# ScalarE in written order in the loop, its normalisation and its decoding cut into parts, weight loads on its queue

## The chip, the cores and the metric

The kernel runs on one core of a Trainium2 chip. The core has a matrix engine (TensorE, PE in the profile, with its weight loads as PEld), a vector engine (VectorE, DVE), a scalar engine (ScalarE, ACT), a general engine (GpSimd, POOL) and a queue engine that mostly issues transfers (SyncE, SP). Each engine takes its instructions in the order of its own queue. The metric is the device time of one execution in microseconds.

## The reference, cut to what matters

Attention with a decay per head (no softmax), then two MLPs; all in float32, the weights come as float64.

```python
scores = scale * np.matmul(q, k.transpose(0, 1, 3, 2))      # 4 x 8 heads, 576 x 64
ret = scores * Dmat[None, :, :, :]                          # gamma ** (i - j), lower triangle
x = np.matmul(ret, v)                                       # -> 2304 tokens x 512

h = x @ w_in                                                # 512 -> 1024
e = np.exp(h - h.max(-1)); sm = e / (e.sum(-1) + 1e-9)
solu = h * sm
ln = (solu - mu) / np.sqrt(var + 1e-6) * g_ln
x = ln @ w_out                                              # 1024 -> 512

h = x @ w_in2                                               # 512 -> 2048
g = np.where(h >= 1, h, np.where(h <= -1, 0.0, (h + 1) ** 2 / 4))
out = g @ w_out2                                            # 2048 -> 512
```

## The kernel before

The 2304 tokens are 18 tiles of 128. Every float32 operand of a product is split into a high part and a low part (`split`, L73: ScalarE copies the high part, VectorE subtracts), and a product is three matmuls.

The program has three stages. **START** is a table of steps that carries the attention ahead by six tiles, prepares the first MLP's weights and begins on the first two tokens' hidden layer. **The loop** (L507) runs over pairs of token tiles a = 2j and a + 1, j = 1 to 8: transposes of the normalised tile a-2 (`mlp1_transpose`, `tp`), scores of the attention of tile ra, the two halves of the hidden layer of tile a (`mlp1_hidden`, `hp`, 12 matmuls each), its normalisation (`mlp1_norm`), the transposes of a-1, the attention output of ra (`ret_out`), the same for a+1, and the first MLP's output of the pair before (`mlp1_out`, `px`). Attention runs until the fifth pair. The text calls j = 1 the first pair, and so on. **The last stage** is the second MLP.

In between, in the loop, the weights of the second MLP are prepared in 32 steps (`prep_w2`): a load of 512 KB (`prep_load`, `st`), `decode` of the float64 words into float32 (ScalarE L197 and L198, VectorE's shift L199, GpSimd's addition L200, VectorE's sign L202), and the split into `wi` (first matrix) or, after two loads, GpSimd's four combinations in `ws` (L366) and the split into `wo` (second matrix, in two parts). The results go to DRAM (`wid`, `wod`) and are loaded again in the last stage. `PACE` says how many steps stand at each of four places of a pair. The stage's loads have three buffers (`st`).

Normalisation of a tile: VectorE takes the two halves' maxima (L255) and their minimum (L261, the maxima are negated); ScalarE exponentiates (`e<-hp`, L265); VectorE multiplies with `hp` (`e<-hp,e`, L266), the last reader of `hp`; ScalarE squares into `junk` (L273); GpSimd takes the power and the bias (L279, L280); ScalarE writes the normalised `e` (L283), which the transposes read. `hp` has two buffers of PSUM (tag "h") in pairs one to five; the odd tiles from 13 on use another tag.

Order: in the loop TensorE and SP are pinned to the written order (L506). VectorE, ScalarE and GpSimd are ordered by a list scheduler.

## Time and profile before

| | |
|---|---|
| runs | 724.83, 729.98, 730.9 us; median 729.98 |
| profiled execution | 727.76 us, of which the span is 726.0 |
| busy: PE, DVE, ACT, POOL | 688.2, 497.1, 359.8, 169.7 us |
| mean granted clock of TensorE | 0.979 |
| START / first pair / pairs two to five / six to eight / last stage | 74.10 / 39.35 / 144.30 / 71.52 / 396.73 us |

TensorE is the busiest engine; busy time is counted over the whole span, and the stages are unlike. A wait counts where the engine that waits is the one that the end depends on. The granted clock is given as a share of 2.4 GHz; 0.5 is 1.2 GHz.

### The profile page before, as it was taken

How to read it: one execution, taken by the hardware profiler on the slowest of the kernel's cores; microseconds unless marked ns; L12 is line 12 of the kernel's file. 1: busy time of each engine (PE TensorE's matmuls, PEld its weight loads, DVE VectorE, ACT ScalarE, POOL GpSimd, SP SyncE). 2: the span in 40 equal slices, each digit the busy share in tenths (PEclk: the TensorE clock that was granted, in tenths of full speed). 3: DMA queues.
4: the chain of work that ended last, by engine and by line, in shares of the span. 5: the costliest groups of instructions: out<-in, count | busy, mean ns of one | idle time of the engine just before them, and what ended most of it. 6: DMA issues, size and time to landing. Idle time of an engine off the chain costs nothing.

```text
span 726.0 us, 12169 instructions
## 1 busy us (share of the span) xinstructions
PE 688.2 (95%) x4744; PEld 618.5 (85%) x4744; DVE 497.1 (68%) x961; ACT 359.8 (50%) x658; POOL 169.7 (23%) x186
## 2 busy tenths in 40 slices
PE   5888789998989999999999999999999999999997
PEld 4677578887878889999888989898988899899996
DVE  2977777677588678754566578556865668575875
ACT  2746775575667569763434344333433343343342
POOL 2896645636555235400000000000000000000000
PEclk9989899999999999999999999999999999999999
DMA  8956534487869399699564523346135511555282
GB/s 299 373 185 250 186 116 157 152 324 245 299 224 340 128 356 394 242 391 402 178 242 143 190 89 144 137 184 218 47 125 192 203 59 59 203 193 196 77 320 116
DMA packets 34825, 152.05 MB, mean 209 GB/s; under 512 B 3792, under 2 KB 11984, under 8 KB 29008
## 3 DMA queue, kind: packets, MB, share of 16 engines
q1 hardware_dynamic: 34624, 151.02, 56.8%
q8 instruction: 37, 0.61, 0.3%
q10 hardware_dynamic: 144, 0.26, 0.1%
q14 instruction: 20, 0.16, 0.1%
HBM read 114.04 MB, written 37.22 MB: 208 GB/s over the span
## 4 chain that ended last, share of the span: by engine, by line
PE 72%; DVE 11%; DMA 6%; ACT 4%; POOL 3%; issue 3%; SPq 0%; DVEq 0%; POOLq 0%; ACTq 0%
PE h L414 27%; PE hp L250 9%; PE px L316 7%; PE pa L462 7%; PE pb L462 7%; PE pc L462 7%; PE pd L462 3%; DMA st<-in_w_out 2%; POOL y L200 2%; PE po L149 1%; DMA wod<-wo 1%; PE tp L296 1%; DVE y L199 1%; DVE wo L75 1%; DVE p L124 1%
## 5 line engine op out<-in xcount | busy, mean ns | idle before, releaser
L414 PE MATMUL h<-xs,wi 128*128 128x512 f32 (+1 forms) x960 | 214.2, 372 | 0.0
L414 PEld LDWEIGHTS h<-xs,wi 128*128 128x128 f32 x960 | 163.8, 188 | 28.5
L424 DVE SCALAR_TENSOR_TENSOR r<-r 128x512 f32<-128x512 f32 (+1 forms) x80 | 50.8, 635 | 104.0 <-ACT r L422 103.9
L422 ACT ACTIVATE r<-h 128x512 f32<-128x512 f32 (+1 forms) x80 | 44.4, 555 | 154.7 <-PE h L414 154.6
L74 ACT ACTIVATE gh<-gs 128x1024 fp32r<-128x1024 f32 (+1 forms) x80 | 66.9, 874 | 77.1 <-DVE gs L437 72.9
L316 PE MATMUL px<-ln,wo 128*128 128x256 f32 x864 | 101.4, 278 | 0.0
L316 PEld LDWEIGHTS px<-ln,wo 128*128 128x128 f32 x864 | 100.5, 188 | 0.8 <-ACT e L265 0.2
L250 PE MATMUL hp<-wi1h,x 128*128 128x512 f32 x288 | 96.3, 417 | 0.0
L75 DVE TENSOR_TENSOR gl<-gs,gh 128x1024 fp32r<-128x1024 f32 (+1 forms) x80 | 77.1, 995 | 13.3 <-ACT gh L74 13.2
L200 POOL TENSOR_TENSOR y<-y,st 128x512 int32<-128x512 int32 x48 | 64.2, 1340 | 70.6 <-ACT st L198 22.9
L250 PE MATMUL hp<-wi1l,x 128*128 128x512 f32 x144 | 62.7, 435 | 14.6 <-DVE e L266 12.6
L462 PE MATMUL pb<-wo,gh 128*128 128x256 f32 x288 | 73.9, 280 | 0.4 <-DVE x L75 0.4
L250 PEld LDWEIGHTS hp<-wi1h,x 128*128 128x128 f32 x288 | 58.6, 203 | 13.4
L437 DVE TENSOR_TENSOR gs<-gs 128x256 f32<-128x256 f32 (+1 forms) x160 | 60.0, 396 | 3.6
L462 PE MATMUL pa<-wo,gh 128*128 128x256 f32 x288 | 62.5, 280 | 0.0
L462 PE MATMUL pc<-wo,gh 128*128 128x256 f32 x288 | 62.0, 280 | 0.0
L429 DVE TENSOR_TENSOR gs<-h,r 128x512 f32<-128x512 f32 (+1 forms) x80 | 51.1, 638 | 7.3 <-DVE r L424 0.5
L462 PEld LDWEIGHTS pb<-wo,gh 128*128 128x128 f32 x288 | 54.3, 188 | 0.6 <-issue 0.6
L462 PEld LDWEIGHTS pa<-wo,gh 128*128 128x128 f32 x288 | 49.2, 189 | 2.7
L462 PEld LDWEIGHTS pc<-wo,gh 128*128 128x128 f32 x288 | 49.1, 188 | 0.0
L250 PEld LDWEIGHTS hp<-wi1l,x 128*128 128x128 f32 x144 | 29.4, 204 | 22.6 <-DVE e L266 13.6
L423 ACT COPY h<-h 128x512 f32<-128x512 f32 (+1 forms) x80 | 43.1, 539 | 0.0
(88 smaller groups left out, 1139.0 us busy)
## 6 DMA issues: line engine op xcount, KB each, us to landing
wo<-wod SPq DMA_DIRECT2D x28, 1792.0 KB, 7.4
wod<-wo SPq DMA_DIRECT2D x8, 1792.0 KB, 9.4
st<-in_w_out SPq DMA_DIRECT2D x24, 512.0 KB, 6.1
qk<-in_qk_t SPq DMA_DIRECT2D x18, 512.0 KB, 6.5
kv<-in_kv SPq DMA_DIRECT2D x18, 512.0 KB, 4.5
xsd<-x SPq DMA_DIRECT2D x36, 256.0 KB, 6.4
st<-in_w_in SPq DMA_DIRECT2D x16, 512.0 KB, 6.2
wid<-wi SPq DMA_DIRECT2D x16, 512.0 KB, 7.2
```

The costliest lines, as they stand in the source:

```text
L74: nc.scalar.activation(hi, src, AF.Copy)
L75: eng.tensor_tensor(out=lo, in0=src, in1=hi.bitcast(F32), op=ALU.subtract)
L200: nc.gpsimd.tensor_tensor(out=y.bitcast(I32), in0=y.bitcast(I32), in1=lo.bitcast(I32), op=ALU.add)
L250: nc.tensor.matmul(hp, a[:, kk, :], w[:, fs], start=(n == 0), stop=(n == 3 * KD - 1))
L316: nc.tensor.matmul(px[:, mm, :], w[:, ms], a[:, f, :], start=(n == 0), stop=(n == 3 * C1 - 1))
L414: nc.tensor.matmul(hp[:, :n], wi[c][:, w, kk], xs[b][:, a, kk], start=(k == 0), stop=(k == 3 * KD - 1))
L422: nc.scalar.activation(r[:, :n], hp[:, :n], AF.Relu, bias=0.5, scale=0.5)
L423: nc.scalar.copy(h[:, :n], hp[:, :n])
L424: nc.vector.scalar_tensor_tensor(out=r[:, :n], in0=r[:, :n], scalar=1.0, in1=r[:, :n], op0=ALU.min, op1=ALU.mult)
L429: nc.vector.tensor_tensor(out=g, in0=h_, in1=r_, op=ALU.max)
L437: nc.vector.tensor_tensor(out=g[:, o], in0=g[:, x], in1=g[:, y], op=op)
L462: nc.tensor.matmul(po[key][:, half], a[:, x, t], wo[p][0][:, w, y], start=(begin and j == 0), stop=(last and j == 2), skip_group_check=True,)
```

## The change

ScalarE is pinned to the written order in the loop too (`order1`), so the order of the text is now its order. For that, three things are rewritten.

1. Normalisation comes in three calls: `norm_exp` (minimum, exponents, `e`), `norm_root` (squares and the power) and `norm_end` (the last ScalarE step). They are spread over a pair: the end of tile a-1 stands at the head of pair a, the end of a after `ret_out(rb)`, the root of a+1 after the first half of the output.
2. `prep_w2` is a pipeline: a call does the last step of one weight (split of `wo`), the sign of the next (and the split of `wi` or the combinations of `ws`), and the scaling and addition (`decode_add`) of the newest. There are two more calls (34), and `PACE` is changed for it. Stores go out one step later.
3. `prep_load` issues on ScalarE's queue instead of SP's, after the step whose sign frees `st`.

START issues the two loads of the mask `inside` between the two loads of the first tile, instead of behind both.

```diff
-PACE = [[], [0, 0, 0, 0], *[[2, 1, 1, 1]] * 4, *[[2, 2, 1, 1]] * 2, [0, 0, 0, 0]]
+PACE = [[], [0, 0, 0, 0], *[[2, 1, 1, 1]] * 2, *[[2, 1, 2, 1]] * 4, [0, 0, 0, 0]]
...
         nc.sync.dma_start(x, qk_t[t])
+        for e in range(2 if t == 0 else 0):
+            load_inside(e)
         nc.sync.dma_start(y, kv[t])
...
+    def norm_root(t):
+        sm, e, nmax, esum, hsum, nmean, sq, rs, nb = norm_cols(t)
         for f in range(2):
             junk = act1.tile([P, 512], BF16, tag="junk", name="junk", bufs=1)
...
+    def norm_end(t):
+        sm, e, nmax, esum, hsum, nmean, sq, rs, nb = norm_cols(t)
         for f in range(2):
             ef = e[:, f * 512 : (f + 1) * 512]
             nc.scalar.activation(ef, ef, AF.Identity, bias=nb, scale=rs)
...
-            nc.sync.dma_start(st, words(w_out2[i * P : (i + 1) * P, :] if w else w_in2[i], DM))
+            nc.scalar.dma_start(st, words(w_out2[i * P : (i + 1) * P, :] if w else w_in2[i], DM))
...
         for _ in range(n):
...
+            a, b = (x.pop(0) if x else None for x in (signed, added))
+            parts = []
+            if a:
+                i, y = a
                 x = prep.tile([P, 2, 7, 2 * P], F32R, tag="wo", name="wo")
                 for part in (slice(0, 4), slice(4, 7)):
-                    split(x[:, 0, part], x[:, 1, part], y[:, part])
-                stores.append((wod[i // 2], x, len(staged) + len(todo)))
+                    hi(x[:, 0, part], y[:, part])
+                    parts.append((x[:, 1, part], y[:, part], x[:, 0, part]))
+                stores.append((wod[i], x, steps[0]))
+            if b:
+                w, i, y, h = b
+                if w == 0:
+                    v = decode_sign(y, h, y)
...
+            if staged:
+                w, i, st = staged.pop(0)
+                added.append((w, i, *decode_add(st)))
+            if b and b[0] == 0:
+                x = prep.tile([P, 2, DM], F32R, tag="wi", name="wi", bufs=2)
+                hi(x[:, 0], v)
...
+            for x in parts:
+                lo(*x)
+            if b:
+                prep_load(1)
+            store_w2(1)
...
     order.enter_context(tc.manual_schedule(engines={nc.tensor.engine, nc.sync.engine}))
+    order1 = ExitStack()
+    order1.enter_context(tc.manual_schedule(engines={nc.scalar.engine}))
...
+        if j > 1:
+            norm_end(a - 1)
+        prep_w2(n[0])
         mlp1_hidden(a, 0)
         mlp1_hidden(a, 1)
-        mlp1_norm(a)
-        prep_w2(n[0])
+        norm_exp(a)
         mlp1_transpose(a - 1)
         if more:
             ret_out(ra)
         prep_w2(n[1])
+        norm_root(a)
...
         mlp1_hidden(a + 1, 1)
-        mlp1_norm(a + 1)
+        norm_exp(a + 1)
...
+        norm_end(a)
         prep_w2(n[2])
...
         mlp1_out(j - 1, 0)
+        norm_root(a + 1)
```

TensorE's order is the same before and after, word for word. The rows below are the queues as the two programs leave them. ScalarE in the second pair, before, from the split (`ln`) of the transposes of tile 2 to the exponents (L265, after the change L276); `st` is the load in decoding, `wi` a weight's split:

```order
L74 ACTIVATE ln<-tp 128x4x128 x2
L283 ACTIVATE e<-e,sm 128x512 x2
L197 ACTIVATE y<-st 128x512
L198 ACTIVATE st<-st 128x512
L74 ACTIVATE wi<-y 128x512
L74 ACTIVATE ln<-tp 128x4x128 x2
L265 ACTIVATE e,sm<-hp,sm 128x512 x2
```

After, the same stretch:

```order
L74 ACTIVATE ln<-tp 128x4x128 x2
L300 ACTIVATE e<-e,sm 128x512 x2
L199 ACTIVATE y<-st 128x512
L200 ACTIVATE st<-st 128x512
L199 ACTIVATE y<-st 128x512
L200 ACTIVATE st<-st 128x512
L377 ACTIVATE wi<-y 128x512
L369 DMA st<-in_w_out 128x1024
L276 ACTIVATE e,sm<-hp,sm 128x512 x2
L74 ACTIVATE ln<-tp 128x4x128 x2
```

Two scalings stand ahead of the exponents where one stood, the exponents ahead of the split of the next transposes instead of behind it, the last normalisation step (L300) at the head, and the loads (L369) between.

VectorE in the fifth pair, before, from the scores' masking (`p`) to `e`:

```order
L124 TENSOR_TENSOR p_2298<-sc_2288,in_sb 128x512
L124 TENSOR_TENSOR p_2300<-sc_2289,in_sb 128x512
L75 TENSOR_TENSOR wo<-ws,wo 128x1024
L75 TENSOR_TENSOR wo<-ws,wo 128x768
L255 TENSOR_REDUCE sm<-hp 128x1 x2
L199 TENSOR_SCALAR y<-y 128x512
L261 TENSOR_TENSOR sm<-sm 128x1
L75 TENSOR_TENSOR ln<-tp,ln 128x4x128 x2
L75 TENSOR_TENSOR wi<-y,wi 128x512
L202 SCALAR_TENSOR_TENSOR y<-st,y 128x512
L266 SCALAR_TENSOR_TENSOR e,sm<-hp,e 128x512 x2
```

After:

```order
L378 TENSOR_TENSOR wo<-ws,wo 128x1024
L378 TENSOR_TENSOR wo<-ws,wo 128x768
L206 SCALAR_TENSOR_TENSOR y<-st,y 128x512
L201 TENSOR_SCALAR y<-y 128x512
L263 TENSOR_REDUCE sm<-hp 128x1
L378 TENSOR_TENSOR wi<-y,wi 128x512
L206 SCALAR_TENSOR_TENSOR y<-st,y 128x512
L263 TENSOR_REDUCE sm<-hp 128x1
L272 TENSOR_TENSOR sm<-sm 128x1
L277 SCALAR_TENSOR_TENSOR e,sm<-hp,e 128x512 x2
L289 TENSOR_SCALAR sm<-sm 128x1
L75 TENSOR_TENSOR ln<-tp,ln 128x4x128
```

`min` (L261) is L272 now, `e` (L266) is L277. The `ln` of the transposes of tile 9 went from in front of `e` to behind it (the second `ln` follows three rows later); a second sign (L206) came in front.

SP at the end of the first pair and into the second, before (`xsd` are the stores of the first MLP's output):

```order
L376 DMA wid_109<-wi 128x1024
L331 DMA xsd_104<-x_1050 128x2x256 x2
L331 DMA xsd_104<-x_1108 128x2x256 x2
L346 DMA st<-in_w_out 128x1024
L376 DMA wid_110<-wi 128x1024
L104 DMA qk<-in_qk_t 128x1024
L105 DMA kv<-in_kv 128x1024
L346 DMA st<-in_w_out 128x1024
L104 DMA qk<-in_qk_t 128x1024
L105 DMA kv<-in_kv 128x1024
L346 DMA st<-in_w_in 128x1024
L376 DMA wod_125<-wo 128x3584
```

After:

```order
L417 DMA wid_109<-wi 128x1024
L353 DMA xsd_104<-x_1040 128x2x256 x2
L353 DMA xsd_104<-x_1108 128x2x256 x2
L417 DMA wid_110<-wi 128x1024
L104 DMA qk<-in_qk_t 128x1024
L107 DMA kv<-in_kv 128x1024
L104 DMA qk<-in_qk_t 128x1024
L107 DMA kv<-in_kv 128x1024
L417 DMA wod_125<-wo 128x3584
```

The loads of `st` are gone from this queue; the stores of the weights, of `x` and the loads of `qk` and `kv` kept their order.

## Rows read from the trace of the kernel before

**Rows 1.** Table by stage: window, length, busy of PE, PEld, DVE, ACT, POOL, clock, DMA

```profile
113.45:149.67 36.22, 33.91 (x259) 30.24 (x258) 23.35 (x53) 19.46 (x38) 17.87 (x22) 0.95 0.55 192
...
186.91:222.38 35.47, 32.92 (x259) 29.50 (x257) 26.01 (x54) 22.28 (x44) 19.57 (x21) 1.00 0.74 262
222.38:257.75 35.37, 33.07 (x251) 29.34 (x250) 24.65 (x52) 21.30 (x42) 12.68 (x15) 0.95 0.61 218
257.75:281.75 24.00, 24.00 (x164) 21.77 (x163) 20.73 (x44) 19.57 (x40) 14.07 (x15) 1.00 0.97 365
...
329.27:726.00 396.73, 390.99 (x2585) 356.33 (x2582) 258.83 (x470) 152.84 (x256) 0.00 (x0) 1.00 0.46 168
```

**Rows 2.** TensorE's waits in the loop (74.1 to 329): total, times, longest

```profile
PE hp L250 <- DVE e L266: 12.6, 5, 2.8
```

**Rows 3.** TensorE in time order: start, length, line, operation, idle before and its releaser

```profile
93.83 1.70 PE L296 MATMUL tp<-ident,e 128*128 128x128 f32 x8 [1.92 <-ACT e L283]
...
121.12 1.03 PE L296 MATMUL tp<-ident,e 128*128 128x128 f32 x8
...
128.56 0.57 PE L250 MATMUL hp<-wi1l,x 128*128 128x512 f32 x1 [2.31 <-DVE e L266]
...
165.21 0.49 PE L250 MATMUL hp<-wi1l,x 128*128 128x512 f32 x1 [2.64 <-DVE e L266]
...
172.46 1.00 PE L143 MATMUL po<-qs,state 128*128 128x64 f32 x8
...
202.36 0.50 PE L250 MATMUL hp<-wi1l,x 128*128 128x512 f32 x1 [2.54 <-DVE e L266]
...
208.06 1.05 PE L143 MATMUL po<-qs,state 128*128 128x128 f32 x8
...
237.49 0.50 PE L250 MATMUL hp<-wi1l,x 128*128 128x512 f32 x1 [2.30 <-DVE e L266]
```

**Rows 4.** SP, ScalarE and VectorE in time order in the second pair

```profile
109.45 7.86 SPq L331 DMA_DIRECT2D xsd<-x  x4
117.41 0.41 SPq L346 DMA_DIRECT2D st<-in_w_out  x1
...
121.93 0.68 ACT L197 ACTIVATE y<-st 128x512 f32<-128x512 f32 x1 [2.43 <-DMA st<-in_w_out]
...
122.64 0.43 DVE L199 TENSOR_SCALAR y<-y 128x512 uint32<-128x512 uint32 x1 [2.60 <-ACT y L197]
```

**Rows 5.** VectorE in time order ahead of the fifth pair's `e`

```profile
233.81 1.27 DVE L75 TENSOR_TENSOR ln<-tp,ln 128x512 fp32r<-128x512 f32 x2
...
235.72 1.09 DVE L202 SCALAR_TENSOR_TENSOR y<-st,y 128x512 uint32<-128x512 uint32 x1
```

**Rows 6.** Groups by line, pairs two to seven: count, busy, mean ns, idle before

```profile
L75 DVE TENSOR_TENSOR wo<-ws,wo 128x1024 fp32r<-128x1024 f32 (+1 forms) x16 | 18.8, 1189 | 2.9 <-ACT wo L74 2.7
...
L75 DVE TENSOR_TENSOR wi<-y,wi 128x512 fp32r<-128x512 f32 x14 | 12.0, 854 | 3.4 <-ACT wi L74 3.3
L202 DVE SCALAR_TENSOR_TENSOR y<-st,y 128x512 uint32<-128x512 uint32 x13 | 11.8, 908 | 3.4 <-POOL y L200 3.4
...
L366 POOL TENSOR_TENSOR ws<-ws 128x256 f32<-128x256 f32 x29 | 23.4, 818 | 14.5 <-DVE ws L202 14.0
```

**Rows 7.** ScalarE's waits in pairs two to seven: total, times, longest

```profile
ACT y L197 <- DMA st<-in_w_in: 16.3, 6, 5.1
```

**Rows 8.** GpSimd in time order in the first pair

```profile
87.49 2.63 POOL L200 TENSOR_TENSOR y<-y,st 128x512 int32<-128x512 int32 x2 [0.42 <-POOL y L200]
90.07 1.01 POOL L279 TENSOR_TENSOR sm<-sm,half 128x1 f32<-128x1 f32 x1
```

**Rows 9.** DMA issues with us to landing; then a load on the chain of waits

```profile
wod<-wo SPq DMA_DIRECT2D x8, 1792.0 KB, 9.4
...
st<-in_w_in SPq DMA_DIRECT2D x16, 512.0 KB, 6.2
...
177.60 7.75 DMA st<-in_w_out
```

More of the change, by code (lines that the diff above doesn't have):

```diff
@@ L339, in net @@
     loads = [(w, i) for p in range(C2 // 2) for w in (0, 1) for i in (2 * p, 2 * p + 1)]
-    todo, staged, stores, ws = list(loads), [], [], {}
+    todo, staged, added, signed, stores, ws = list(loads), [], [], [], [], {}
+    steps = [0]
     def prep_load(n):
@@ L351, in prep_w2 @@
         for _ in range(n):
-            w, i, st = staged.pop(0)
-            later = [x for x in stores if len(staged) + len(todo) <= x[2] - 2]
-            stores[:] = [x for x in stores if x not in later]
-            if w == 0:
-                x = prep.tile([P, 2, DM], F32R, tag="wi", name="wi", bufs=2)
-                split(x[:, 0], x[:, 1], decode(st))
-                stores.append((wid[i], x.rearrange("p w (c f) -> p w c f", c=KD), len(staged) + len(todo)))
-            elif i % 2 == 0:
-                ws[i // 2] = prep.tile([P, 7, 2 * P], F32, tag="ws", name="ws")
-                decode(st, dst=ws[i // 2][:, 0:2].rearrange("p i f -> p (i f)"))
-            else:
-                y = ws.pop(i // 2)
-                decode(st, dst=y[:, 2:4].rearrange("p i f -> p (i f)"))
-                for o, a, b in ((4, 1, 0), (1, 3, 1), (5, 3, 4), (6, 2, 5)):
-                    nc.gpsimd.tensor_tensor(out=y[:, o], in0=y[:, a], in1=y[:, b], op=ALU.subtract)
+            steps[0] += 1
@@ L379, in net, with store_w2 @@
+            store_w2(1)
+    def store_w2(age):
+        for x in [x for x in stores if x[2] <= steps[0] - age]:
+            nc.sync.dma_start(x[0], x[1].bitcast(F32))
+            stores.remove(x)
     xs, gs, ghl, wi, wo, po = {}, {}, {}, {}, {}, {}
@@ L574, in net @@
     store_x2()
+    order1.close()
     mlp1.close()
```

49 lines of the change are left out of this document (34 added, 15 removed).

## The prediction

> **What bounds the kernel now.** I read the table by stage first. After 329.27 the kernel is a stage of 396.73 us in which TensorE is busy for 390.99 [rows 1]; nothing of the change reaches into it, so only what lies before can move. In the pairs with attention the table shows something else: the second pair of the loop takes 36.22 us with TensorE busy for 33.91 at a granted clock of 0.95, the fourth 35.47 with 32.92 at 1.00, while the sixth, which has no attention, is 24.00 us long and TensorE busy for all of it [rows 1]. The loss is in the pairs one to five. The list of TensorE's waits names it in one line: the matmuls of `hp` wait for VectorE's `e` (L266), 5 times, 12.6 us in all [rows 2]. In time order [rows 3] there is one such wait in each of the pairs two to five, always ahead of the first matmul of token a+1's first half: 2.31, 2.64, 2.54 and 2.30 us. (The fifth, 2.8, the longest, is in the first pair, where the loop's pattern has only begun; I leave it as it is.) The first pair adds a wait of another kind, 1.92 us of the transposes for ScalarE's last normalisation step, L283 [rows 3].
>
> The reason is a buffer: `hp` has two slots, so token a+1's first half needs that of token a, which is free when `e` (L266) has read it. Without the wait that half would start at 128.56 - 2.31 = 126.25, which is 12.8 us after the pair's start at 113.45; in the fifth pair 237.49 - 2.30 = 235.19, again 12.8 after its start at 222.38. So **12.8 us after the start of a pair is the due time of the first `e`**, and the change is worth what it does to that one due time.
>
> A wait costs more than itself. The 24 matmuls of `hp` behind the wait take 172.46 - 165.21 = 7.25 us in the third pair and 208.06 - 202.36 = 5.70 in the fourth [rows 3]. The stages say the same: 0.95 granted in the second pair, 1.00 in the fourth [rows 1]. So after four of the five waits TensorE ran part of the next stretch at 1.2 GHz instead of 2.4, and I put 1.55 us for that to each of the pairs one, two, three and five, none to the fourth.
>
> **What the change gives back.** Waits: 1.92 + 2.31 + 2.64 + 2.54 + 2.30 = 11.71. Clock: 4 x 1.55 = 6.20. Together 17.9 us, if all five go. Part by part, why I think they go:
>
> *Second pair.* ScalarE's decode step (L197) came at 121.93 after waiting 2.43 for a load; that load was issued at 117.41 by SP, whose queue had stood from 109.45 for 7.86 us on the stores of `x` [rows 4]. VectorE's shift (L199) waited for ScalarE another 2.60, and the reduction of the second half, which the exponent and so `e` need, stood behind it, though TensorE had gone on from that half to the transposes at 121.12 [rows 3]. So here a wait for a load travelled through two engines into TensorE. After the change the load is on ScalarE's queue, issued two decode steps ahead of its use, and VectorE has `min` and both `e` ahead of the two `ln` of the next transposes, where `ln`, a sign and a `wi` stood before. Walking the new order with durations as in [rows 6], each instruction at the latest of its operands and of its predecessor, I get the first `e` done some 10.8 us after the pair's start: due time kept with about 2 us in hand.
>
> *Third pair.* Same walk: 12.0, some 0.8 in hand. *Fourth pair.* Before, ScalarE stood 5.1 for a load [rows 7]; that load is issued earlier now; 11.2, so 1.6 in hand. *Fifth pair.* Before, two `ln` from 233.81, a `wi` and a sign from 235.72 for 1.09 stood ahead of `e` with the exponent long done [rows 5]. The `ln` go behind `e`, but two halves of `wo` (2 x 1.19), two signs (2 x 0.91) and a `wi` (0.85) stand ahead of it [rows 6]: 5.05 us of decode on VectorE, where before it was 2.38 + 0.85 + 0.91 = 4.14. The walk, in us from the pair's start: GpSimd's four combinations (0.82 each) end at 6.65, ScalarE's second half of `wo` and VectorE's follow, VectorE's first sign starts at 8.35, its second shift at 9.0, then a reduction and the `wi`, the second sign at 10.7, the reduction at 11.4, `min` 12.1, the exponent 12.15, `e` 12.85 to 13.55. That is 0.8 late; I count 1.0, between 0 and 2. *First pair.* GpSimd had two additions of the decode at 87.49 for 2.63 us in front of the power of token 1's normalisation at 90.07 [rows 8]; in the new code no decode for the second MLP is pulled up into this stretch, since ScalarE's written order has it later. I count the 1.92 and its clock as gone.
>
> **What it adds.** (a) 32 issues of loads move from SP's queue to ScalarE's. An issue on SP took 0.41 [rows 4], so 0.8 us go onto ScalarE between the start of a pair and the exponent when two steps stand there; that is in the walk. ScalarE waits for nothing but the slot of `st`, which its own step two places before and GpSimd's addition free. (b) ScalarE can no longer step around a late operand: behind a decode step that waits for its load stand the exponent and all that follows. The trace of before shows what such a wait is: 6 waits of 16.3 us for loads of the first matrix, the longest 5.1 [rows 7]. The loads now have two steps of lead, about 7 to 9 us, against a median of 6.2 from issue to landing [rows 9]; one on the chain took 7.75 [rows 9]. Taken at nothing, bounded by rival C. (c) Two more steps of decode (34 for 32) and stores one step later: the stores land in DRAM long before the stage that reads them; in pairs four and five the third place has two steps where it had one, behind the due `e`. In pairs six and seven there is no wait for `hp` to win, and two steps ahead of the exponent push the split of the transposes back, which the first `px` needs; for that in the seventh I take 1.0 us, between 0 and 2. (d) The two loads of the mask that move in START swap places with one load of equal use: nothing, within 0.5 either way.
>
> The Trainium skill's page "DMA: Bandwidth & Descriptors", section "Issuing engines are not separate DMA queues", says that transfers of all issuers share the same 16 engines, and that a second issuer saves only the sequencer's time to start them. By that alone, moving 32 loads would be worth 32 x 0.41 = 13 us of SP's own time and nothing on the path; the second pair's wait would stay, with 2.31 + 1.55 = 3.9 us, and the sum would be 717. The trace disagrees in the case that counts: SP's 7.86 us were no start of a transfer but a queue that stood still with a load behind it [rows 4].
>
> **Sum.** The profiled execution took 727.76, of which 726.0 are the span. 727.76 - 17.9 + 1.0 (fifth pair) + 1.0 (seventh) = 711.9. The median of the three runs is 729.98, 2.2 above the profiled one, so on the median's scale 714.1; since the first pair's other wait, 2.8, may shorten as well once ScalarE does not decode there, by 0 to 2, I take 1 for it and say **713**.
>
> **The rivals.**
> A. *VectorE is the bound in the pairs that carry a `wo`.* ScalarE is in order, but VectorE is still ordered by the scheduler, and in pairs three and five its queue in front of `e` is as long as it was. For: 5.05 against 4.14 us of decode in the fifth pair, 0.8 in hand in the third. Against: `ln` leaves the front in both. Price: the waits and the clock of two pairs stay, 2.64 + 1.55 + 2.30 + 1.55 = 8.0, less the 1.0 counted: 713 + 7 = 720.
> B. *The gain does not come.* The waits are replaced by as many others: exponents on time, but normalisation's end or the transposes late, since ScalarE must take every step in its place. Price: the five waits stay, at other lines: 727 to 731. Against: the last normalisation step of the odd token now stands at the head of the pair, and the transposes that need it come 7.5 us later.
> C. *Slower: ScalarE stands in order for loads.* The second decode step at the head of a pair uses a load issued at the end of the pair before, some 8 us ahead, and the exponent stands behind it. Beyond that and the slack of about 1.3 each microsecond of lateness goes into TensorE. If a load is as late again as in the worst wait of before, 5.1 [rows 7], a pair waits 5.1 - 1.3 = 3.8 and loses 1.55 of clock behind it; in the pairs two to seven that is 6 x 5.35 = 32 us on top of 713: 745. The sign turns where six pairs lose the 17.9 again: 3.0 each, 1.4 of it wait, so from a landing of about 8 + 1.3 + 1.4 = 10.7 us on. For: a store of 1792 KB, at work beside the loads, has a median of 9.4 [rows 9]. Against: the loads' own median of 6.2 [rows 9].
> The Trainium skill, same page, "Anatomy of one DMA", says that a semaphore wait is made by the issuing sequencer ahead of the dispatch; it bears on C, since the issue of a load that waits for its slot now holds up ScalarE. No row of before shows such a wait on ScalarE.
>
> **How the numbers follow.** A measurement of this kernel tells 1% from no change (7.3 us). Forecast (709 to 717) 0.56; A (717 to 722.6) 0.18; B 0.15; C 0.09; better than 709, with the wait of 2.8 gone too and no residue, 0.02. So faster by over 1%: 0.76; within 1%: 0.15; slower 0.09. For a range that leaves out no more than 2 in 10, I go from 705 (all residues zero, the wait of 2.8 and its clock gone: 714.1 - 2.0 - 2.8 - 1.55 = 707.8, less 0.4% between runs) up to 726 (A, and most of the lower half of B).
>
> **What would show it.** In the profile after: TensorE's wait for `e` drops from 5 times to one or two, the pairs two to four come to 32 to 33 us with a clock of 1.00, the fifth to 33 to 34; the last stage stays at 396 to 397. ScalarE's wait for `st` loads should be under 5 us in all. If that wait grows over 15 and stands ahead of the exponent, C holds; if VectorE's `e` comes late with ScalarE's exponent long done, A. The prediction is wrong if the pairs two to five keep their length, or if the last stage moves.

## The result and the profile after

The changed kernel takes 734.79 us in the median (732.53 to 735.97, 11 runs), the kernel before 726.91 in runs beside it: ratio 1.0108, 95% interval 1.0083 to 1.0133. The forecast was 713. The profiled execution has a span of 733.0 us, 7.0 more than before.

The table by stage of the changed kernel, cut where a pair's first transposes start (window, length, busy time of PE, PEld, DVE, ACT, POOL, granted clock, DMA share, GB/s):

```profile
73.94:110.21 36.27, 30.12 (x174) 26.18 (x173) 18.64 (x49) 20.18 (x42) 10.47 (x13) 0.91 0.20 71
110.21:142.91 32.70, 32.70 (x259) 29.52 (x258) 24.85 (x51) 19.61 (x40) 15.40 (x18) 1.00 0.58 200
142.91:181.72 38.81, 35.59 (x259) 31.47 (x258) 30.55 (x59) 23.48 (x45) 21.44 (x24) 0.91 0.65 233
181.72:214.56 32.84, 32.84 (x258) 29.49 (x257) 29.20 (x59) 22.68 (x46) 16.89 (x18) 1.00 0.69 253
214.56:252.83 38.27, 33.21 (x250) 29.54 (x249) 28.29 (x53) 22.27 (x44) 20.96 (x21) 0.96 0.88 326
252.83:282.07 29.24, 26.14 (x163) 23.43 (x162) 25.52 (x47) 22.24 (x42) 15.35 (x15) 0.94 0.75 272
282.07:312.45 30.38, 25.96 (x163) 23.14 (x162) 23.69 (x50) 23.14 (x46) 15.08 (x19) 0.94 0.78 284
...
336.13:733.00 396.87, 391.15 (x2586) 356.52 (x2584) 258.81 (x470) 154.28 (x258) 0.00 (x0) 1.00 0.47 172
```

Length before and after in us, both counted from the start of a pair's first transposes. (In [rows 1] the sixth pair ends at 281.75; these transposes start at 281.59, so the sixth is 23.84 long here and the last stage 396.89.)

| START | pair 1 | 2 | 3 | 4 | 5 | 6 | 7 | 8 | last stage |
|---|---|---|---|---|---|---|---|---|---|
| 74.10 | 39.35 | 36.22 | 37.24 | 35.47 | 35.37 | 23.84 | 23.84 | 23.68 | 396.89 |
| 73.94 | 36.27 | 32.70 | 38.81 | 32.84 | 38.27 | 29.24 | 30.38 | 23.68 | 396.87 |

START and the pairs one, two and four win 0.16 + 3.08 + 3.52 + 2.63 = 9.4; the pairs three, five, six and seven lose 1.57 + 2.90 + 5.40 + 6.54 = 16.4. The last stage stays. TensorE in time order names the losses; these rows answer to [rows 3] (start, length, line, operation, idle before and its releaser; L258 is the old L250, L338 the old L316, L318 the old L296):

```profile
159.02 0.79 PE L258 MATMUL hp<-wi1l,x 128*128 128x512 f32 x1 [3.22 <-DVE e L277]
...
218.62 1.53 PE L117 MATMUL sc<-qk 64*128 64x128 f32 x16 [3.02 <-DMA qk<-in_qk_t]
...
234.05 0.50 PE L258 MATMUL hp<-wi1l,x 128*128 128x512 f32 x1 [2.04 <-DVE e L277]
...
269.15 13.08 PE L338 MATMUL px<-ln,wo 128*128 128x256 f32 x96 [3.10 <-DVE ln L75]
...
284.32 0.66 PE L318 MATMUL tp<-ident,e 128*128 128x128 f32 x4 [1.65 <-DVE x L75]
...
299.82 1.41 PE L338 MATMUL px<-ln,wo 128*128 128x256 f32 x10 [2.77 <-DVE ln L75]
```

The second and fourth pair have no wait at all now. The third still waits for `e`. The fifth has a wait for the load of `qk` and a second one for `e`. The sixth and seventh, full before, wait for VectorE's split of the transposes (`ln`) ahead of `px`, and for the split of `px` itself (`x`). The 96 matmuls of `px` then take 13.08 and 12.79 us, against 11.05 each in the same pairs of before; the granted clock of these pairs is 0.94, so part of that stretch ran at 1.2 GHz. The sixth pair of before:

```profile
270.70 11.05 PE L316 MATMUL px<-ln,wo 128*128 128x256 f32 x96
```

What stands behind the third pair's wait: ScalarE, then VectorE, then GpSimd in time order.

```profile
156.28 0.63 ACT L377 ACTIVATE wi<-y 128x512 fp32r<-128x512 f32 x1 [5.78 <-DVE y L206]
...
156.82 0.67 ACT L276 ACTIVATE e<-hp,sm 128x512 f32<-128x512 f32 x1
...
149.22 2.09 DVE L378 TENSOR_TENSOR wo<-ws,wo 128x1024 fp32r<-128x1024 f32 x2
...
152.75 1.53 DVE L201 TENSOR_SCALAR y<-y 128x512 uint32<-128x512 uint32 x1
...
154.81 1.44 DVE L206 SCALAR_TENSOR_TENSOR y<-st,y 128x512 uint32<-128x512 uint32 x1
156.17 0.56 DVE L272 TENSOR_TENSOR sm<-sm 128x1 f32<-128x1 f32 x1
...
158.28 0.68 DVE L277 SCALAR_TENSOR_TENSOR e<-hp,e 128x512 f32<-128x512 f32 x1
...
152.37 1.62 POOL L202 TENSOR_TENSOR y<-y,st 128x512 int32<-128x512 int32 x1 [6.79 <-DVE y L201]
```

ScalarE stood 5.78 us at `wi`, the high part of a weight, and the exponent stands behind it in the written order. That `wi` needs VectorE's sign of the step before it, the sign needs GpSimd's addition, and the addition needs VectorE's shift. The second shift of the two steps in a row, 0.42 us elsewhere, took 1.53 and ended at 154.28, just behind the addition that ran from 152.37 to 153.99; the sign behind it took 1.44. The same exponent also needs VectorE's minimum (L272), which ended at 156.73, when ScalarE was about done with `wi` (the exponent starts at 156.82). VectorE had no idle time from 145.61 until `e`, and the two subtractions of `wo` stood on it ahead of all these steps. So two things end together here, `wi` on ScalarE and the queue on VectorE, and these rows alone do not say what taking away one of them would give.

Behind the fifth pair's first wait: SP, and the VectorE step that its first row waited for.

```profile
207.87 0.33 SPq L417 DMA_DIRECT2D wod<-wo  x1
208.87 0.33 SPq L417 DMA_DIRECT2D wid<-wi  x1
209.36 1.14 SPq L104 DMA_DIRECT2D qk<-in_qk_t  x1
...
205.75 2.10 DVE L378 TENSOR_TENSOR wo<-ws,wo 128x1024 fp32r<-128x1024 f32 x2 [0.26 <-ACT wo L377]
```

The load of `qk` was issued at 209.36, behind stores of `wo` and `wi` that wait for VectorE's splits; TensorE got it at 218.62, 9.3 us later. In the kernel before the same load went out 29.7 us ahead of the fifth pair's start (222.38):

```profile
192.73 0.38 SPq L104 DMA_DIRECT2D qk<-in_qk_t  x1
```

In the sixth pair the split of the transposes stands behind the exponents, and these behind VectorE's minimum, which came late (ScalarE, then VectorE):

```profile
265.65 0.69 ACT L276 ACTIVATE e<-hp,sm 128x512 f32<-128x512 f32 x1 [3.59 <-DVE sm L272]
...
267.00 1.08 ACT L74 ACTIVATE ln<-tp 128x512 fp32r<-128x512 f32 x2
...
268.42 1.28 DVE L75 TENSOR_TENSOR ln<-tp,ln 128x512 fp32r<-128x512 f32 x2
```

### The profile page after: what moved, and what is told of

Its sections match the earlier page's. It is cut to its first block, busy times and chain, and to the rows that moved or that the text cites. A ratio compares the mean times of both kernels' runs of the same rounds, so it can differ in the third digit from the quotient of the medians.

```text
span 733.0 us, 12147 instructions
## 1 busy us (share of the span) xinstructions
PE 689.6 (94%) x4744; PEld 620.2 (85%) x4744; DVE 504.0 (69%) x961; ACT 359.4 (49%) x658; POOL 170.1 (23%) x186
## 4 chain that ended last, share of the span: by engine, by line
PE 58%; DVE 3%; issue 1%; ACT 1%; POOL 0%; DVEq 0%; ACTq 0%
PE h L456 27%; PE pa L504 7%; PE pb L504 7%; PE pc L504 7%; PE px L338 4%; PE pd L504 3%; PE hp L258 2%; PE tp L318 1%; DVE gl L75 1%; DVE wi L378 0%; DVE osb L534 0%; DVE wo L378 0%; ACT gh L74 0%; DVE y L201 0%; POOL y L202 0%
## 5 line engine op out<-in xcount | busy, mean ns | idle before, releaser
L338 PE MATMUL px<-ln,wo 128*128 128x256 f32 x864 | 105.1, 284 | 5.9 <-DVE ln L75 5.9
L338 PEld LDWEIGHTS px<-ln,wo 128*128 128x128 f32 x864 | 103.9, 194 | 7.4 <-DVE ln L75 6.8
L258 PE MATMUL hp<-wi1h,x 128*128 128x512 f32 x288 | 94.6, 411 | 0.0
L258 PE MATMUL hp<-wi1l,x 128*128 128x512 f32 x144 | 61.4, 426 | 11.4 <-DVE e L277 8.0
L258 PEld LDWEIGHTS hp<-wi1h,x 128*128 128x128 f32 x288 | 57.3, 199 | 12.8
L258 PEld LDWEIGHTS hp<-wi1l,x 128*128 128x128 f32 x144 | 28.8, 200 | 19.3 <-DVE e L277 8.7
L276 ACT ACTIVATE e<-hp,sm 128x512 f32<-128x512 f32 x36 | 24.3, 682 | 39.6 <-DVE sm L272 39.6
```

The lines of the kernel that those rows point to most:

```text
L258: nc.tensor.matmul(hp, a[:, kk, :], w[:, fs], start=(n == 0), stop=(n == 3 * KD - 1))
L276: nc.scalar.activation(ef, hp, AF.Exp, bias=nmax, scale=1.0, accum_out=sm[:, 3 + f : 4 + f])
L338: nc.tensor.matmul(px[:, mm, :], w[:, ms], a[:, f, :], start=(n == 0), stop=(n == 3 * C1 - 1))
```

## The experiments

Theories as the expectations name them. **P**: each loss has a place, something that stands on a pinned queue ahead of what is due. **T**: the transfer of `qk` itself is late. **Q**: the pin costs. **V**: VectorE has too much ahead, wherever things stand. **L**: decode in three steps puts VectorE beside GpSimd, which stretches it. **W**: work moved out of the first pair into full ones. **D**: two decode steps in a row. **WO**: a step that splits `wo` at a pair's head (such a step has two high parts on ScalarE and two subtractions on VectorE beside the usual). Every ratio is to the kernel before on the same chip.

**e1_qk_early**: the loads of `qk` and `kv` ahead of the decode steps.

```diff
+        if more and ra + 2 < NT:
+            load_qkv(ra + 2)
         prep_w2(n[2])
-        if more and ra + 2 < NT:
-            load_qkv(ra + 2)
```

(and likewise for rb + 2 and the last place)

> The changed kernel with the loads of the next attention tiles (qk, kv) written ahead of the decode steps of the third and fourth place, so that SP does not stand at a weight's store with them behind it. Nothing left out. Theory P (the losses have places: here the load of qk stood on SP behind a store that waits for VectorE's wo): the wait of 3.0 us for qk at the head of the fifth pair goes, and 1.5 of clock behind it; GpSimd is no longer held at qs by the same load, so the wait of 2.0 for e goes or shrinks too: the fifth pair 38.3 -> 32 to 33, the whole 728 to 730. Theory T (the transfer itself is late, since the DMA engines are full): the wait stays within 1 us, 734 to 736.

726.53 us, ratio 0.9994 (0.9967 to 1.0020): 8.3 below the changed kernel and level with before. Its fifth pair:

```profile
210.18:243.39 33.21, 31.43 (x251) 28.19 (x250) 27.24 (x55) 23.31 (x45) 19.92 (x21) 1.00 0.92 340
```

38.27 became 33.21 and the wait for `qk` is gone; T falls. 1.78 of waiting for `e` stayed, so GpSimd's `qs` was the smaller part of that. The first pair was 3.2 us shorter as well, at a granted clock of 1.00 instead of 0.91; no edit touches it, and I do not count it as an effect, though some of the 8.3 may be it. So the first pair can differ by 3 us between two profiles by its clock.

**e3_split_first** (from the changed kernel): the exponents of the even tile behind the transposes in the pairs six to eight.

```diff
-        norm_exp(a)
+        if j < 6:
+            norm_exp(a)
         mlp1_transpose(a - 1)
+        if j >= 6:
+            norm_exp(a)
```

> The changed kernel with the exponents of the even tile written behind the split of the transposes of the odd one in the pairs six to eight, where no buffer of hp waits for them. Nothing left out. Theory P: the waits of px for ln (3.1 and 2.8) and the clock behind them (13.1 and 12.8 against 11.1 us for 96 matmuls) go: the sixth pair 29.2 -> 25 to 26, the seventh 30.4 -> 25 to 26, the whole 725 to 728. Theory V (VectorE has too much ahead, in whatever order ScalarE delivers): the split of VectorE stays late, at most 2 us come back, 733 to 735.

737.05 us, ratio 1.0142 (1.0111 to 1.0173). TensorE in the sixth and seventh pair:

```profile
267.44 11.58 PE L338 MATMUL px<-ln,wo 128*128 128x256 f32 x96 [1.00 <-DVE ln L75]
...
284.85 1.11 PE L318 MATMUL tp<-ident,e 128*128 128x128 f32 x4 [5.39 <-DVE x L75]
...
298.92 1.33 PE L338 MATMUL px<-ln,wo 128*128 128x256 f32 x9
```

`px` waits 1.00 and no longer at all, but the transposes wait 5.39 for `x`. The predicted places are right and the time did not come back: the next thing on the same queue was late.

**e4_not_pinned** (from the changed kernel): `order1` is not entered.

> The changed kernel without the pin of ScalarE: its order in the loop is left to the scheduler, all else (parts of the normalisation, decode in three steps, loads on its queue) as changed. Nothing left out. Theory Q (the pin itself costs, since ScalarE cannot step around a late operand): pairs three, five, six and seven come back to 37, 35, 24, 24 or less, the whole 712 to 728. Theory P: the scheduler reorders by its own costs and brings other waits; the gain of pairs two and four (3.5 and 2.6) is lost with it, the whole 725 to 740.

737.17 us, ratio 1.0141 (1.0110 to 1.0172). Q falls as the whole cause: without the pin TensorE's waits for `e` in the loop are 10.0, those for `x` grow from 1.6 to 5.4, those for the normalisation's end (5.0) are new, and the time is no better. In part it holds: the third pair is 36.83 long and the seventh 24.00, so these two losses go with the pin, and with it go the gains of the first (39.71), second (35.81) and fourth pair (37.18).

**e5_loads_on_sp** (from the changed kernel): `nc.scalar.dma_start` of the weight loads is `nc.sync.dma_start`.

> The changed kernel with the weight loads issued by SP as before. Nothing left out. Theory P: the queue is not what won pairs two and four (the exponents ahead of the splits and loads two steps ahead did) nor what lost the others: 732 to 738, pairs two and four within 1.5 us of the changed kernel's 32.7 and 32.8. Rival: the queue took the loads out from behind the stores of x; back on SP they are late, ScalarE in order waits for them, 740 to 760.

735.44 us, ratio 1.0126 (1.0084 to 1.0167); the pairs two and four are 32.27 and 33.09 long. In all the queue neither won nor lost: the gain of those pairs is the order's. In the fifth pair it moved a wait: 7.08 us for `qk` and none for `e`, where the changed kernel has 3.02 and 2.04.

**f1_one_at_head**, **f2_head_split** (both from e1): one step at the head of a pair; f2 has e3's edit too.

```diff
-*[[2, 1, 1, 1]] * 2, *[[2, 1, 2, 1]] * 4
+*[[1, 2, 1, 1]] * 2, *[[1, 2, 2, 1]] * 4
```

> The kernel of e1_qk_early (726.5) with one decode step instead of two at the head of every pair, the other behind the exponents of the even tile (the four places carry 1, 2, 1, 1 and 1, 2, 2, 1 steps). Nothing left out. Theory P (what stands on ScalarE ahead of the exponent and of the transposes' split decides): the wait for e in the third pair (2.7, and 3.2 in the changed kernel) and its clock go, -4; the waits for ln in the sixth and seventh (2.3 and 3.0) and their clock go, -4 to -8; the whole 714 to 719. Theory V (VectorE, ordered by the scheduler and held by GpSimd, has as much ahead either way): the waits move to x or px and 722 to 730 stay.

> As f1_one_at_head, and in the pairs six to eight the exponents of the even tile behind the split of the transposes of the odd one. Nothing left out. Theory P: no wait for ln is left in the pairs six and seven, 1 to 3 us below f1. Theory V: as e3_split_first showed, the time turns up as a wait of the transposes for x in the seventh pair (5.4 there), 0 to 4 us above f1.

739.57 (1.0184, 1.0137 to 1.0232) and 737.97 (1.0175, 1.0135 to 1.0215): both slower than e1 by over 11 us. TensorE's waits in f1:

```profile
PE tp L318 <- DVE x L75: 10.3, 4, 4.0
```

The waits of `px` for `ln` went and 10.3 us for `x` came. P as stated, that the head alone decides, falls: the two steps in a row went from the head to the second place, and the waits came behind that place. The third pair did gain: with one step at its head, the one that splits `wo`, its wait for `e` is 1.18 instead of 2.69, and it is 34.92 long instead of 38.54.

**f3_vector_pinned**, **f4_vector_head**: VectorE pinned to the written order too, on e1 and on f1.

> The kernel of e1_qk_early with VectorE pinned to the written order in the loop as ScalarE is. Nothing left out. Theory V (the scheduler puts signs, shifts and weight splits of VectorE ahead of min and e, and of the splits of x): pairs three, six and seven lose their waits at least in part, 715 to 722. Theory P: VectorE in written order has the whole decode of the pair's head ahead of min, and waits with it for GpSimd's additions: 727 to 745.

> As f3_vector_pinned, with one decode step at the head of a pair as in f1_one_at_head. Nothing left out. Theory P: half the decode ahead of the exponent on both engines, 712 to 722, below f3. Theory V: as f3 within 3 us.

751.43 (1.0360, 1.0317 to 1.0402) and 757.62 (1.0448, 1.0402 to 1.0495). f3 misses V's range by 29 us. VectorE's order by the scheduler is not what loses; in written order it is worse, in f3 with one wait of 10.34 us for `e`.

**g1_first_pair**, **g2_first_pair_6** (both from e1): four and six steps in the first pair, the first three loads by SP at its head.

```diff
+        if j == 1:
+            prep_load(3, nc.sync)
...
-PACE = [[], [0, 0, 0, 0], *[[2, 1, 1, 1]] * 2, *[[2, 1, 2, 1]] * 4, [0, 0, 0, 0]]
+PACE = [[], [0, 0, 2, 2], *[[2, 1, 1, 1]] * 6, [0, 0, 0, 0]]
```

(the `prep_load(3)` further down in the first pair goes; g2: `[0, 1, 2, 3]`, then four times `[2, 1, 1, 1]` and twice `[1, 1, 1, 1]`)

> The kernel of e1_qk_early (726.5) with four of the 34 decode steps done in the first pair (0, 0, 2, 2; all later pairs 2, 1, 1, 1), their first three loads issued by SP at the head of that pair. Nothing left out. Theory W (work moved: the scheduler of before did about six of the 32 steps in the first pair, where the engines had room; the written order does none there, and the pairs three to seven carry them, above all VectorE in six and seven, whose 49.2 us of work are more than the 47.7 they had): the first pair grows by 0 to 2, the waits of the sixth and seventh pair shrink, each 30 -> 25 to 27, the whole 715 to 722. Theory L (the decode in three steps puts VectorE's passes beside GpSimd's additions, which stretches them, wherever the steps stand): what goes from the late pairs comes back in the first, 724 to 730.

> As g1_first_pair with six steps in the first pair (0, 1, 2, 3), the pairs two to five 2, 1, 1, 1 and the sixth and seventh 1, 1, 1, 1. Nothing left out. Theory W: the sixth and seventh pair at 24 to 25, as before the change; the whole 2 to 4 us below g1 unless the first pair gets a wait of its own: 711 to 719. Theory L: as e1, 724 to 730.

724.17 (0.9947, 0.9922 to 0.9972) and 723.39 (0.9955, 0.9930 to 0.9980). In g2 the second pair and the sixth and seventh:

```profile
107.40:148.91 41.51, 34.80 (x259) 31.26 (x257) 34.97 (x66) 27.43 (x52) 26.61 (x29) 0.92 0.79 292
...
252.34:276.18 23.84, 23.84 (x162) 21.61 (x161) 18.47 (x43) 19.23 (x39) 11.59 (x12) 1.00 0.82 299
276.18:300.02 23.84, 23.84 (x162) 21.60 (x161) 17.35 (x40) 16.71 (x34) 10.26 (x11) 1.00 0.43 166
```

With four steps each the sixth and seventh are full again, as W said; but the second pair is 41.51 long, since the last three steps of the first pair stand ahead of its transposes' split. g1 has 30.60 in the seventh pair with VectorE busy for 20.91 of it, no more than in before's 23.84 (20.98). So amount alone does not explain the seventh. By the times alone g1 lies in L's range and g2 just below it, and both miss W's.

**g3_before_held**: the kernel before, with `store_x2()` ahead of `prep_load(3)` in the first pair, so that no weight is decoded early.

> The kernel before, with the stores of the first half of the pair's output put ahead of the first loads of the second MLP's weights in SP's queue, so that no weight of it can be decoded in the first pair. Nothing left out, and no engine is pinned that was not. Theory W: the first pair loses its wait and is 2 to 4 us shorter, the pairs from three on are longer by more, the sixth and seventh are no longer full: 730 to 740, as slow as the changed kernel without any of its edits. Theories P and L: the loss is in the new order, so before keeps its time or gains the first pair's wait: 722 to 728.

724.16 us, ratio 0.9969 (0.9949 to 0.9989). The first pair is 32.96 long, the second:

```profile
107.23:145.04 37.81, 34.37 (x258) 30.71 (x257) 34.39 (x61) 25.66 (x50) 27.00 (x25) 0.95 0.78 281
```

W's mirror fails. The work left the first pair and the scheduler put it into the second and third (37.81 and 37.55 long); the sixth and seventh stay at 23.84 each, and the kernel is if anything a little faster.

**h1_split_first**, **h2_places**: g1 with e3's edit; h2 in addition with 0, 1, 2, 2 in the first pair, 1, 2, 1, 1 in two and three, 2, 1, 1, 1 in four to six, 1, 1, 1, 1 in the seventh.

> The kernel of g1_first_pair (724.2) with the exponents of the even tile behind the split of the transposes of the odd one in the pairs six to eight. Nothing left out. Theory P (a step on ScalarE holds up what is written behind it): the wait of px for ln in the seventh pair (4.0) shrinks by the two exponents, 1.3 to 2 us, and the 0.9 of the sixth goes; what is left is the second step's wi, which waits for VectorE's sign and still stands ahead; the clock behind it (13.7 against 11.1 us for px) comes back in part: 719 to 722. Theory V (VectorE alone): unchanged, 723 to 726.

> As h1_split_first with the steps at other places: 0, 1, 2, 2 in the first pair, 1, 2, 1, 1 in the second and third, 2, 1, 1, 1 in the fourth to sixth, 1, 1, 1, 1 in the seventh (34 in all). Nothing left out. Theory P: the waits for e of the second and third pair (2.8 and 2.4 in g1) shrink to 0 to 1.2, as f1 had them, and the seventh pair is full at 23.8 as in g2: 708 to 715. Theory V: the waits move to x or to the transposes: 718 to 726.

723.13 (0.9956, 0.9931 to 0.9980) and 720.11 (0.9910, 0.9884 to 0.9936). Both are in V's ranges and not in P's. In h1 the seventh pair waits 4.47 for `ln`, no less than in g1 (3.97). ScalarE, VectorE and GpSimd there:

```profile
284.34 0.63 ACT L377 ACTIVATE wi<-y 128x512 fp32r<-128x512 f32 x1 [3.70 <-DVE y L206]
...
280.79 1.55 DVE L201 TENSOR_SCALAR y<-y 128x512 uint32<-128x512 uint32 x1
...
282.87 1.45 DVE L206 SCALAR_TENSOR_TENSOR y<-st,y 128x512 uint32<-128x512 uint32 x1
...
280.34 1.72 POOL L202 TENSOR_TENSOR y<-y,st 128x512 int32<-128x512 int32 x1 [5.70 <-DVE sm L272]
282.48 1.28 POOL L202 TENSOR_TENSOR y<-y,st 128x512 int32<-128x512 int32 x1 [0.42 <-issue]
```

`wi` (284.34) waited 3.70 for a sign, with the split of the transposes behind it (284.88). The second shift took 1.55 beside the first step's addition, and the second addition could only start at 282.48. ScalarE's side of the third pair's picture is here again, and it gave D.

**k1_apart** (from g1): no two steps in a row in the pairs two to seven, as many in each pair as in g1.

```diff
         mlp1_transpose(a - 1)
+        prep_w2(n[1])
         if more:
             ret_out(ra)
-        prep_w2(n[1])
         norm_root(a)
+        prep_w2(n[2])
...
-PACE = [[], [0, 0, 2, 2], *[[2, 1, 1, 1]] * 6, [0, 0, 0, 0]]
+PACE = [[], [0, 0, 0, 2, 2], *[[1, 1, 1, 1, 1]] * 6, [0, 0, 0, 0, 0]]
```

(the later two places are n[3] and n[4])

> The kernel of g1_first_pair (724.2) with no place in the pairs two to seven that has two decode steps in a row: the second step of the head stands behind the exponents of the even tile and the split of the transposes, the next behind the squares (1, 1, 1, 1, 1; the first pair's four steps as in g1). As many steps in every pair as in g1, nothing left out. Theory D (what loses is two steps in a row: the second one's wi on ScalarE has to wait for shift, addition and sign of the first, on VectorE and GpSimd, and the exponent and the split stand behind it): the waits for e in the second and third pair (2.8, 2.4) and for ln in the sixth and seventh (0.9, 4.0) go, each under 1; 706 to 714. Theory W (the number of steps in the pair decides): as g1, 721 to 726.

716.26 us, ratio 0.9866 (0.9835 to 0.9896): the fastest here, ahead of both kernels, and 2 us above D's range. Second, third, sixth and seventh pair:

```profile
107.90:141.04 33.14, 32.42 (x258) 29.10 (x257) 29.19 (x57) 22.72 (x46) 19.22 (x20) 1.00 0.65 234
141.04:179.68 38.64, 35.69 (x259) 31.53 (x258) 30.68 (x58) 24.03 (x47) 26.06 (x28) 0.91 0.83 302
...
243.91:267.75 23.84, 23.84 (x163) 21.61 (x162) 18.29 (x40) 18.16 (x36) 10.94 (x11) 1.00 0.74 279
267.75:293.06 25.31, 24.71 (x162) 21.92 (x161) 19.57 (x46) 20.96 (x44) 12.98 (x17) 1.00 0.80 311
```

33.14, 23.84 and 25.31 where g1 had 36.71, 25.06 and 30.60. In the seventh the heads differ in nothing but the second step: both split `wo` there, and the wait ahead of `px` went from 3.97 to 0.57, as D says. In the second and sixth a `wo` left the head along with the second step, so these two do not tell D from WO. The third pair is longer than in g1 (35.43), and its wait for `e` is 2.95, so D does not explain it. Its exponent waited for VectorE, in time order:

```profile
149.01 1.23 DVE L378 TENSOR_TENSOR wo<-ws,wo 128x1024 fp32r<-128x1024 f32 x1 [0.55 <-ACT wo L377]
...
150.75 1.44 DVE L378 TENSOR_TENSOR wo<-ws,wo 128x768 fp32r<-128x768 f32 x1
152.11 1.26 DVE L201 TENSOR_SCALAR y<-y 128x512 uint32<-128x512 uint32 x1
...
154.61 0.52 DVE L272 TENSOR_TENSOR sm<-sm 128x1 f32<-128x1 f32 x1
```

Two subtractions of `wo` and a shift that took 1.26 stand ahead of the minimum (154.61).

Since k1 has the steps per pair of g1, and the decode in three steps, neither V nor L can be the whole loss. A part for L is not ruled out: the 32 shifts on VectorE took 19.8 us in g1 and 17.4 in k1. But they took 22.2 in e1, which is 8 us faster than the changed kernel with 21.2.

**k2_apart_late** (from e1): the same for the head alone, with none in the first pair; one double place (the fourth) is left in the pairs four to seven.

> The kernel of e1_qk_early (726.5) with the two steps of a pair's head set apart in the same way (1, 1, 1, 1, 1 in the pairs two and three, 1, 1, 1, 2, 1 in four to seven; none in the first pair), as many steps in every pair as there. Nothing left out. Theory D: the waits for e of the third and fifth pair (2.7, 1.8) and for ln of the sixth and seventh (2.3, 3.0) go; the two steps in a row that are left stand ahead of the split of px, so the wait of the transposes for x (1.4) stays or grows: 712 to 722. Theory W: the late pairs have six steps each as before, 724 to 730.

732.70 us, ratio 1.0083 (1.0051 to 1.0115). TensorE's waits:

```profile
PE tp L318 <- DVE x L75: 6.8, 3, 2.9
PE hp L258 <- DVE e L277: 6.0, 2, 3.2
PE tp L318 <- ACT wi L377: 3.3, 1, 3.3
```

The waits for `ln`, 5.3 in e1, are gone, as D said; the waits for `x` grew from 1.4 to 6.8 at the double place that is left, and the transposes wait 3.3 for ScalarE. The third pair's wait for `e` did not go (3.25), as in k1. The time missed both theories' ranges; I read it so that with all 34 steps in six pairs no place is left that is not ahead of something due, which no run shows.

**m1_wo_before**, **m2_wo_second**, **m3_wo_to_four** (all from k1): where `wo` is split, moved against the third pair.

```diff
-PACE = [[], [0, 0, 0, 2, 2], *[[1, 1, 1, 1, 1]] * 6, [0, 0, 0, 0, 0]]
+PACE = [[], [0, 0, 0, 2, 2], [1, 1, 1, 1, 2], [1, 1, 1, 0, 1], *[[1, 1, 1, 1, 1]] * 4, [0, 0, 0, 0, 0]]
```

(m1; m2 has `[1, 1, 1, 0, 1]` and `[1, 1, 1, 1, 2]` in the second and third pair; m3 has `[0, 0, 0, 1, 2]` in the first and `[1, 1, 1, 1, 2]` in the seventh)

> From k1_apart (716.3 us, third pair 38.6 long with 2.95 of waiting for e), one step moved: 1, 1, 1, 1, 2 in the second pair and 1, 1, 1, 0, 1 in the third, so that the step which splits wo stands at the end of the second pair and no longer at the head of the third. WO (the wait goes with a split of wo at a pair's head, whose two subtractions on VectorE stand ahead of the reductions): the third pair's wait for e falls under 1.0 and it is 34 to 36.5 long; the second, with two steps at its end, 33 to 35.5; the time is 713 to 717. AMOUNT (the third pair has too many steps for VectorE, wherever wo stands): the same fall here, but the opposite in m2. ELSE (neither): wait 2 to 3.5 again, 716 to 718.

> From k1_apart, one step moved the other way: 1, 1, 1, 0, 1 in the second pair and 1, 1, 1, 1, 2 in the third, so that wo is split at the third pair's second place, and the pair has one step more. WO: the wait for e ahead of the third pair's second hidden row falls under 1.0 although the pair has six steps; its length is 35 to 38, with what VectorE then is late with (x or ln) at no more than 2.5; the time is 713 to 718. AMOUNT: the wait for e stays at 2.5 to 4.5 and the pair is 39 to 42 long, 717 to 721.

> From k1_apart, one step of the first pair moved to the end of the seventh, so every step in between comes one place later: wo is split at the head of the fourth pair (and not of the third and seventh), with five single steps in each of the pairs two to six as before. WO: the third pair's wait for e falls under 1.0 (34 to 36.5 long) and the fourth, with 32.9 and no wait in k1_apart, gets one of 1.5 to 4 (35 to 37.5 long). AMOUNT or ELSE: the third pair keeps 2.5 or more and the fourth has none. The time is 714 to 719 by either, since one wait moves and the seventh pair has a step more.

717.58 (0.9893, 0.9835 to 0.9952), 722.87 (0.9966, 0.9933 to 1.0000) and 719.29 (0.9915, 0.9885 to 0.9945): none beats k1, and m1 cannot be told from it. m3 is the clean one, five single steps in both pairs in question. TensorE at the second hidden tile of its third and fourth pair:

```profile
154.84 0.51 PE L258 MATMUL hp<-wi1l,x 128*128 128x512 f32 x1 [0.91 <-DVE e L277]
...
190.11 0.50 PE L258 MATMUL hp<-wi1l,x 128*128 128x512 f32 x1 [0.65 <-DVE e L277]
```

In the third pair 2.95 became 0.91, as WO said, and the pair is 3.1 shorter (35.54). In the fourth 0.65 came, not 1.5 to 4, and it is 33.56 long: a `wo` at the head costs something there too, but much less, and f1's third pair (1.18) and h2's second (0.73) with the same single step at the head agree with that. m2 lies between the two theories, 1.94 and 36.18 long with six steps. m1 missed: there is no wait for `e`, but 5.33 ahead of the odd tile's transposes, since the step that splits `wo` now follows at once, at the second pair's end, on the step that completes its words:

```profile
153.58 2.28 PE L318 MATMUL tp<-ident,e 128*128 128x128 f32 x8 [5.33 <-DVE ln L75]
...
144.82 0.84 ACT L377 ACTIVATE wo<-ws 128x768 fp32r<-128x768 f32 x1 [3.08 <-POOL ws L399]
```

m2 has the same at the third pair's end, and a wait of 4.81 behind it in the fourth. These two are D again at another place, with the `wo` step as the second of the two.

## Why the prediction was wrong

**The first, second and fourth pair, the last stage, the queue.** Right: forecast gains of 3.47, 3.86 and 2.54, measured 3.08, 3.52 and 2.63; the last stage did not move. For the first pair the close agreement is luck: its clock alone moves it by 3 us, as e1 shows, and its other wait, of which 1 us was counted as gone, is 2.76 before and after. That the queue is not what wins is shown by e5. Rival C, weight loads that land too late, did not happen: ScalarE's waits for loads in the pairs two to seven were 20.5 us before and are one of 1.6 now.

**Where the sum went wrong.** The third, fifth, sixth and seventh pair each came out 5.4 to 5.8 us worse than their terms: gains of 4.19 and 2.85, nothing and a loss of 1.0 were forecast, losses of 1.57, 2.90, 5.40 and 6.54 came. These four are nearly the whole miss.

**The step that failed first: the walk of the third pair.** It put the first `e` 12.0 us after the pair's start. It was done at 158.96, 16.0 after 142.91, and 3 us after its due time. Only the walk's result is on record, with durations as in [rows 6], so which of its instructions came out too early cannot be said. What the trace shows in its place is VectorE at work without a gap from 145.61, with `wo`, a shift of 1.53 and a sign of 1.44 us ahead of the minimum, where [rows 6] have 0.91 for a sign; and on ScalarE a `wi` that waited 5.78 for that sign. I had noticed the rule (behind a step that waits stand the exponent and all that follows) but applied it to loads alone, and put the slower case on rival C only. Rival A had the right engine for this pair, at 8 us for two pairs; B, every step in its place, is nearest to what happened, at 727 to 731.

**The fifth pair: "stores one step later", taken at nothing.** The walk itself was near: with the load of `qk` out of the way (e1) `e` is 1.78 late, where 1.0 between 0 and 2 was counted, and the pair 33.21 long, where 33 to 34 was forecast. What failed is the term for the stores. The store of `wo` waits for VectorE, and on SP the load of the next attention tile stands behind it. Counted from the split, the code writes a weight's store one step behind, where it was two steps before, and the fourth pair has two steps at the third place; so the store of the first one's `wo` comes ahead of the load. e1 shows what the place of the load costs: 5.1 us in the fifth pair. Which of the two changes to the stores put it there, no run separates.

**"For the first `px` of the seventh pair 1.0, between 0 and 2", and nothing in the sixth.** They cost 6.5 and 5.4. Those pairs were full and so had nothing to win, and I priced only what they might lose there by one number without a walk. What the seventh loses is two steps in a row ahead of the split that `px` needs: g1 against k1 shows it with the number of steps and the place of `wo` unchanged (30.60 to 25.31), while one step less, e1 against g1, gave nothing (30.42 to 30.60, with `wo` moved from the head's second step to its first). ScalarE's wait for a sign ahead of that split is seen in g1 (2.31 us) and h1 (3.70); in the changed kernel's seventh pair it is not there, and VectorE's own queue holds up `ln`. The sixth went from 28.26 in e1 to 25.06 in g1 with one step less and to 23.84 in k1 with the steps apart; `wo` moved as well in both, so the share of each is not shown.

**The first pair's decoding.** I counted its absence there as a gain and wrote down no place where the same work would turn up. g1 and g2 show that the pinned order wants it there; g3 shows that a free order does without. So it is not the cause by itself.

**The third pair's rest.** Its wait for `e` is 2.64 before and 3.22 after. Rival A named the mechanism, VectorE with a `wo` ahead of the reductions. m3 shows it for k1: with the same number of steps the wait fell from 2.95 to 0.91 when `wo` left the head. In the order of the changed kernel the second step has a part too, as f1's third pair shows (2.69 in e1, 1.18 there, with `wo` at the head in both). What makes `wo` dearer in k1's third pair than in m3's fourth is argued from rows: the minimum starts 13.57 after the pair's start in k1 and 11.25 in m3, 2.32 later. Of that 1.05 is `norm_end`, which waits for GpSimd (5.46 against 4.41 after the start); 0.51 is the subtractions (2.67 against 2.16 in all) and 0.85 the shift (1.26 against 0.41), both beside GpSimd's scalings, which came later in k1 because GpSimd's scaling of `qk` waited for its load until 149.05.

**Open**: why a single step with `wo` at the head costs 0.7 to 1.6 us of waiting in some pairs and about 3 in the third pair of k1 and k2; and what a steady plan without any such place would give. The fastest kernel still has the third pair at 38.64 against 32.85 for a pair without a wait, and no version tried here had all of them full.

## What to carry to other kernels

When an engine is pinned to a written order, walk each instruction that stands ahead of a due one back through all engines that it waits for, not only its loads. In a pipeline whose step goes round three engines, two steps in a row on the pinned engine cost time wherever something due stood behind them: the same number of steps, apart, gave 716.3 instead of 724.2 us here, part of it from the place of the heaviest step. Walk the other engines' queues as well: an instruction that is due can be held up on two of them at once. And a saving at one due time is worth nothing until the full stretches have been walked as well: the two pairs without any wait lost more than the first two pairs won.

## What the runs showed of the hardware

VectorE's shift of 128x512 words in SBUF takes 0.42 us and up to 1.55 beside an addition or a scaling on GpSimd; in three cases it ended 0.28 to 0.29 us behind the end of GpSimd's instruction (154.28 and 153.99 in the changed kernel, 282.34 and 282.06 in h1, 153.37 and 153.09 in k1's third pair). The reductions from PSUM kept their 0.68 beside it. The Trainium skill, "SBUF — State Buffer", section "SBUF: two separate sides", says that where VectorE's instruction runs in a mode with two ports or reads two inputs from SBUF, it and GpSimd's share a pair of ports as an exclusive lock held for a whole instruction, and that the other then blocks. The ends of these rows agree with such a block; the mode of the shift is not in them. In the changed kernel the 32 shifts took 21.2 us against 14.7 before, 6.5 us on VectorE that no count of instructions shows.
